# Twenty more score banks on VectorE, early memsets and a new instruction order in a two-layer attention and mixer kernel

## The chip, the cores and the metric

The kernel runs on one core of a Trainium2 chip. The metric is device time in microseconds (us) of one execution; the median of several executions is given. Five engines work side by side, each through its own list of instructions in order, and wait for each other by semaphores: PE (TensorE, matmuls; PEld is its weight load), ACT (ScalarE), DVE (VectorE), POOL (GpSimd) and SP (SyncE, which here only issues DMAs).

## The reference

The same layer is applied twice to a 2048 x 448 matrix: attention with 16 heads of 28 columns, then a mixer of two small feed-forward steps.

```python
def _A_ref(x, wqkv, wo):                 # S = 2048, D = 448, H = 16, Dh = 28
    qkv = (x @ wqkv).reshape(B, S, 3, H, Dh).transpose(2, 0, 3, 1, 4)
    q, k, v = qkv[0], qkv[1], qkv[2]
    p = softmax(einsum("bhqd,bhkd->bhqk", q, k) * Dh ** -0.5)
    return einsum("bhqk,bhkd->bhqd", p, v).transpose(0, 2, 1, 3).reshape(B, S, D) @ wo

def _B_ref(x, w1, w2, w3, w4):
    h = gelu(layernorm(x) @ w1)
    # four column groups of h, shifted by -1, +1, -2, +2 rows, side by side: hs
    x1 = x + hs @ w2
    return x1 + gelu(layernorm(x1) @ w3) @ w4     # w3: 448 x 1792

for _ in range(2):
    x = x + _A_ref(layernorm(x), wqkv, wo)
    x = x + _B_ref(layernorm(x), w1, w2, w3, w4)
```

## The kernel before

**Tiling.** The 2048 rows are 16 tiles of 128. The attention goes by *units* of 512 query columns: four in the first layer, three of 512 and two of 256 in the second. A unit is worked off in *segments*, one for each of four groups of four heads (the first unit of layer 0 and the first two of layer 1 also go by three parts of the keys). The work of a segment is cut into *score banks*: a PSUM bank with 128 keys by 512 scores of one head. PE fills a bank with scores (`L1441`, K=32 rows, one matmul, or two of 256 columns in the halved units), the exponential of the bank is taken, and PE multiplies it with V (`L1511`) into one accumulating bank. There are 2048 banks in the two layers.

**Two ways for the exponential.** Most banks go to ACT, three and two banks in turn to one ACTIVATE (a *granule*, `L1484`, 128x1536 and 128x1024). Five of the eight PSUM banks hold scores for ACT, so PE can be at most one granule ahead of it. The table `SHARE` says how many banks of each segment go to DVE instead: `t_ditem` computes their exponential with five instructions (`L1396`, `L1402`, `L1407`, `L1409`, `L1412`), from a score bank made by `L1392` to a bf16 tile `dT`. `SHARE` has 116 of the 2048 banks.

**Everything else lies between.** LayerNorm (statistics on DVE, `rstd` on POOL), K, Q and V projections (`wk_pad`, `wq_pad`, `wv`), the norms of q and k (`sq` with `astat`; the squares mostly on POOL, `L1105`), the output projection (`wo_pad`), and the mixer (`w` with `xT` is w1 or w3, `w` with `hT` is w2, `w` with `h2T` is w4) are split into strips of 32 output rows on PE (`Columns.matmul`, `L174`), so that four of them run side by side in the array. Gelu (`L1674`, `L1817`) is on ACT and needs another function table than the exponential, so a table load stands before and after each block of gelus. Filler matmuls (`wk_pad` with `zero` or `ident`) keep PE's clock up.

**What sets the order.** The program is written as some hundred Python generators that yield operations. A list scheduler (`Sched`) lays each engine's instructions in one fixed order, from its own table of durations: a first pass gives each operation a latest start, which is its rank; `reorder` shifts ranks at random by the entries of `SEEDS`, a list of numbers and tuples (about 1050 entries), and a second pass picks by these ranks. On the chip each engine then runs its list in order; only semaphores make it wait. A change in `SEEDS` therefore moves instructions everywhere, and none of its entries can be read by itself.

**The start.** The input is loaded twice: a bf16 copy in a weight buffer (`w`), for the first four tiles, and `x_res` (`L866`, four DMAs from POOL's queue: POOL itself issues them). For the first four tiles DVE computes statistics (`L984`, `L986`, `L990`), POOL `rstd` (`L992`), DVE the normalized rows `xn` (`L1075`), PE transposes them. `t_setup2` (`L957` to `L969`) clears buffers on POOL: `xn` pads, `vaug` (the padded V with its column of ones), `wo_pad`, and the last rows of `w1` and `w3`. The maximum of the norms (`L930` to `L939`, `sc`) is needed before the scaled q (`L1134`). The first ACT exponential follows.

## Time and profile before

| what | us |
|---|---|
| median of 3 runs | 1063.17 (1063.0 to 1063.62) |
| profiled execution | 1062.37 |
| its span on the core | 1060.3 |
| first exponential on ACT starts | 33.48 |
| last exponential on ACT ends | 1014.14 |
| ACT busy | 1003.3 |
| PE busy | 986.8 |
| DVE busy | 840.9 |
| POOL busy | 161.2 |

The span is what lies between the first and the last instruction of the profiled execution; its own time is 2.07 us more, and the median of the runs is 0.8 us above that execution. "Busy" counts the time in which an engine executes something other than waits and issues; matmuls are pipelined, so PE's figure is an upper bound of what it needs. In the rows below, the number in front of a timeline row is its start, the next its length; the bracket at its end tells how long the engine had idled and who released it; a row with "x5" is a group of neighbours on one line. A row with "busy, mean ns" is a group over the whole span. Rows of a table by windows have for each engine the busy time in that stretch and, in brackets, the instructions.

### The profile page before, as it was taken

What the parts mean: (1) busy time and instruction counts of PE and PEld (TensorE: products, weight loads), DVE (VectorE), ACT (ScalarE), POOL (GpSimd) and SP (SyncE); (2) the same over time, 40 slices, a digit from 0 to 9 for tenths busy, and PEclk for the clock granted to TensorE, in tenths of its full rate; (3) what the DMA queues carried; (4) which work ended last, traced back from release to release, by engine and by line L of the source; (5) the groups of instructions that cost most, each with busy time, mean ns of one, the idle gap of its engine ahead of it and who ended that gap; (6) DMA issues with size and microseconds to landing.
All of it is one profiled execution on the core that took longest, in us unless ns stands there. A gap on an engine that the chain in (4) does not pass through costs nothing.

```text
span 1060.3 us, 31768 instructions
## 1 busy us (share of the span) xinstructions
PE 986.8 (93%) x14218; PEld 390.6 (37%) x14219; DVE 840.9 (79%) x1854; ACT 1003.3 (95%) x908; POOL 161.2 (15%) x177
## 2 busy tenths in 40 slices
PE   7999999999999998999998999999999999999898
PEld 5333333333333333333334333333333333443355
DVE  8999999999968775754996689999988788545463
ACT  5899999999999999999699999999999999999954
POOL 5220101210202002100332012001112020120111
PEclk9999999999999999999999999999999999999999
DMA  7222060100000000101112222010011010010000
GB/s 203 61 74 74 25 179 22 22 16 2 22 21 22 2 21 23 21 2 42 32 51 67 75 67 72 22 42 21 11 32 37 2 34 12 22 27 25 12 19 23
DMA packets 77103, 41.26 MB, mean 39 GB/s; under 512 B 61288, under 2 KB 70376, under 8 KB 76968
## 3 DMA queue, kind: packets, MB, share of 16 engines
q1 hardware_dynamic: 74856, 35.58, 12.9%
q0 software_dynamic: 2112, 3.67, 1.4%
q8 instruction: 111, 1.82, 0.7%
q14 instruction: 24, 0.20, 0.1%
HBM read 14.20 MB, written 8.13 MB: 21 GB/s over the span
## 4 chain that ended last, share of the span: by engine, by line
ACT 73%; PE 22%; DVE 4%; issue 0%; DMA 0%; POOL 0%; DVEq 0%; ACTq 0%
ACT PT L1484 66%; PE ps L174 11%; PE ps L1441 5%; PE ps L1511 3%; ACT h2T L1817 3%; PE ps L1796 1%; ACT hT L1674 1%; PE ps L1822 1%; ACT L1484 1%; DVE xn L1075 1%; ACT L1674 1%; DVE st L984 0%; DMA w<-in_A_x_dram 0%; DVE qT L1134 0%; DVE sc L935 0%
## 5 line engine op out<-in xcount | busy, mean ns | idle before, releaser
L1484 ACT ACTIVATE PT<-ps 128x1536 bf16<-128x1536 f32 (+1 forms) x775 | 879.5, 1259 | 14.4 <-PE ps L1441 13.0
L1441 PE MATMUL ps<-qT,kT 32*128 32x512 bf16 (+1 forms) x2184 | 303.0, 359 | 30.8 <-ACT PT L1484 24.9
L1511 PE MATMUL ps<-PT,vaug 128*32 128x512 bf16 (+1 forms) x2184 | 233.0, 360 | 5.1 <-ACT PT L1484 3.5
L1441 PEld LDWEIGHTS ps<-qT,kT 32*128 32x128 bf16 x2184 | 76.0, 91 | 253.9 <-ACT PT L1484 147.0
L174 PE MATMUL ps<-xT,w 128*32 128x512 bf16 (+5 forms) x2324 | 150.6, 345 | 1.0 <-DVE h2T L1805 0.4
L1805 DVE CAST h2T<-ps 128x512 bf16<-128x512 f32 (+2 forms) x126 | 73.7, 585 | 40.5 <-PE ps L174 38.2
L1511 PEld LDWEIGHTS ps<-PT,vaug 128*32 128x32 bf16 x2184 | 61.9, 94 | 108.9 <-issue 53.8
L174 PE MATMUL ps<-w,h2T 128*32 128x448 bf16 x1524 | 94.3, 354 | 6.6 <-ACT h2T L1817 3.0
L1396 DVE TENSOR_SCALAR dT<-ps 128x512 f32<-128x512 f32 x116 | 79.1, 684 | 14.8 <-PE ps L1392 11.3
L174 PE MATMUL ps<-wk_pad,zero 128*32 128x256 bf16 x1644 | 81.0, 275 | 0.0
L1407 DVE SCALAR_TENSOR_TENSOR dU<-dF 128x512 f32<-128x512 uint16 x116 | 79.3, 684 | 0.9
L1412 DVE SCALAR_TENSOR_TENSOR dT<-dU,dT 128x512 int32<-128x512 f32 x116 | 79.4, 685 | 0.8
L1409 DVE SCALAR_TENSOR_TENSOR dU<-dF,dU 128x512 f32<-128x512 uint16 x116 | 79.1, 682 | 0.7
L174 PEld LDWEIGHTS ps<-xT,w 128*32 128x32 bf16 (+1 forms) x2324 | 53.0, 95 | 53.2 <-issue 24.6
L1825 DVE SCALAR_TENSOR_TENSOR x_res<-x_res,mst,ps 128x448 f32<-128x448 f32 x32 | 21.6, 678 | 61.2 <-PE ps L174 48.2
L1105 POOL TENSOR_TENSOR sq<-qT 128x512 bf16<-128x512 bf16 (+1 forms) x32 | 31.9, 999 | 248.9 <-DVE qT L1091 191.7
L1764 POOL TENSOR_TENSOR x_res<-x_res,x1b 128x448 f32<-128x448 f32 x31 | 37.2, 1204 | 184.7 <-DVE x1b L1745 183.2
L174 PEld LDWEIGHTS ps<-w,h2T 128*32 128x32 bf16 x1524 | 38.1, 96 | 43.4 <-issue 15.3
L1105 POOL TENSOR_TENSOR sq<-kT 128x512 bf16<-128x512 bf16 (+1 forms) x32 | 31.7, 991 | 137.3 <-DVE kT L1091 90.9
L1402 DVE TENSOR_SCALAR dF<-dT 128x512 uint16<-128x512 uint16 x116 | 48.5, 418 | 0.6
L174 PEld LDWEIGHTS ps<-wk_pad,zero 128*32 128x32 bf16 x1644 | 40.0, 95 | 23.8 <-issue 19.1
L1817 ACT ACTIVATE h2T<-h2T 128x3584 bf16<-128x3584 bf16 (+2 forms) x18 | 46.9, 2605 | 0.3
(172 smaller groups left out, 1189.3 us busy)
## 6 DMA issues: line engine op xcount, KB each, us to landing
uscr<-u_sb SPq DMA_DIRECT2D x24, 256.0 KB, 2.1
uin<-uscr SPq DMA_DIRECT2D x24, 256.0 KB, 2.8
x_res<-in_A_x_dram POOLq DMA_DIRECT2D x4, 896.0 KB, 5.3
out_dram<-uin SPq DMA_DIRECT2D x16, 112.0 KB, 1.7
w<-in_B_w_dram SPq DMA_DIRECT2D x1, 1568.0 KB, 13.4
w<-in_B_w_dram SPq DMA_DIRECT2D x1, 1344.0 KB, 8.6
h2T<-in_A_wqkv_dram SPq DMA_DIRECT2D x2, 336.0 KB, 4.5
xT<-xn SPq DMA_TRANSPOSE x33, 3.7
```

What stands on the lines that cost most here:

```text
L174: return [self.e.matmul(out=out[c:min(c + 32, self.m)], lhsT=lhsT[:, c:min(c + 32, self.m)], rhs=rhs, start=start, stop=stop, tile_positio ...
L1105: yield op("pool", 0.1 + 0.002 * nw, lambda e, si=si: e.tensor_tensor(out=sq[:, si, 0:nw], in0=dst, in1=dst, op=ALU.mult), reads=dkeys, wr ...
L1396: yield op("dve", c_ps(cw), lambda e, b=b: e.tensor_scalar(out=dT[:, s, 0:cw], in0=ps[:, bi(b), 0:cw], scalar1=65536.0 + 127 * 128.0, scal ...
L1402: yield op("dve", c_f2b(cw), lambda e: e.tensor_scalar(out=dF[:, f, 0:cw], in0=dT[:, s, 0:cw].bitcast(U16).rearrange("p (q two) -> p q two ...
L1407: yield op("dve", c_ps(cw), lambda e: e.scalar_tensor_tensor(out=dU[:, v, 0:cw], in0=dF[:, f, 0:cw], scalar=-16384.0, in1=dF[:, f, 0:cw], ...
L1409: yield op("dve", c_ps(cw), lambda e: e.scalar_tensor_tensor(out=dU[:, v, 0:cw], in0=dF[:, f, 0:cw], scalar=EXPD * 16384.0, in1=dU[:, v, 0 ...
L1412: yield op("dve", c_ps(cw), lambda e: e.scalar_tensor_tensor(out=dT[:, s, 0:cw].bitcast(I32), in0=dU[:, v, 0:cw], scalar=EXPC * 2.0 ** -35 ...
L1441: yield op("pe", 0.012 + W / 2400.0, lambda e, bk=bk, r0=32 * j, g=g, kc=kc, q0=q0, W=W, c0=W * h: e.matmul(out=ps[:, bk, c0:c0 + W], lhsT ...
L1484: yield op("act", e_dur(n), lambda e, b0=b0, p0=p0, cnt=cnt, cw=cw: e.activation(out=PT[:, p0:p0 + cnt, 0:cw], in_=ps[:, b0:b0 + cnt, 0:cw ...
L1511: yield op("pe", 0.004 + nt * 0.0133, lambda e, j=j, rhs=rhs, vs=vs, i=i: e.matmul(out=ps[32 * j:32 * j + 32, bi(SUM), 0:128 * nt], lhsT=v ...
L1805: yield op("dve", c_ps(NW), lambda e, fch=fch, b=b: e.tensor_copy(out=h2T[:, fch, hoff:hoff + NW], in_=ps[:, bi(b), 0:NW]), reads=[("ps", ...
L1817: yield op("act", c_act(7 * NW), lambda e, f0=f0: e.activation(out=h2T[:, f0:f0 + 7, hoff:hoff + NW], in_=h2T[:, f0:f0 + 7, hoff:hoff + NW ...
```

## The change

There are four parts. `SHARE` gives one more bank of each segment to DVE in the third unit of both layers, two more in the fourth unit of layer 0 and one more in the fourth (a halved one) of layer 1: 4 + 8 + 4 + 4 = 20 banks, 136 for 116. Three POOL memsets (`vaug` twice, `wo_pad`) move from `t_setup2` into a task of their own, `t_pads`, that is started with the first operations. The tasks that load `x_res` start after the first `xn` rows in the scheduler's order instead of after `rstd`, the clearing of the `xn` pads too, and that of `w1` and `w3` after `RTN` (`L871` of the changed kernel, a step of the maximum of norms); three memsets lose the mark `nolk`, which only the scheduler's model reads. `SEEDS` is replaced by another list, of about 330 entries. The signals are of the scheduler only; on the chip no semaphore is added by them.

```diff
     SEEDS = [
-        (3033793134, 1, 35, -35.9), 510908, 684737, (3033793134, 1, 0, -0.4), (3017015515, 1, 0, -39.1), 562618, 531615, 486769, 672476,
...
+        229462, 345458, 889503, (3033793134, 1, 0, -1.6), 467902, 545934, 474656, (3000237896, 1, 0, 32.7), 711263, 951096, 905249, 9256,
...
-    SHARE = {0: {(0, 0): 0, (0, 1): 1, (0, 2): 3, 1: 6, 2: 4, 3: 2}, 1: {(0, 0): 0, (0, 1): 1, (0, 2): 3, (1, 0): 0, (1, 1): 1, (1, 2): 3, 2: 4, 3: 1, 4: 0}}
+    SHARE = {0: {(0, 0): 0, (0, 1): 1, (0, 2): 3, 1: 6, 2: 5, 3: 4}, 1: {(0, 0): 0, (0, 1): 1, (0, 2): 3, (1, 0): 0, (1, 1): 1, (1, 2): 3, 2: 5, 3: 2, 4: 0}}
...
             yield ("spawn", t_warm(), 2)
+            yield ("spawn", t_pads(), 2)
             yield ("spawn", t_load(ld_x, last), 2)
...
+        def t_pads():
+            yield op("pool", 1.2, lambda e: e.memset(vaug[:, :, :].rearrange("p t (h r) -> p t h r", r=32)[:, :, :, 28:32], 0.0), writes=[("vaug_all",)], nolk=1)
+            yield op("pool", 1.5, lambda e: e.memset(vaug[:, :, :].rearrange("p t (h r) -> p t h r", r=32)[:, :, :, 28:29], 1.0), writes=[("vaug_all",)], nolk=1)
+            yield ("sig", ("vinit",))
+            yield op("pool", 1.9, lambda e: e.memset(wo_pad[:, :, :], 0.0), writes=[("wo_pad",)], nolk=1)
...
         def t_load(ld_x, after):
-            yield ("wait", ("rstd0",))
+            yield ("wait", ("xn0",))
...
         def t_setup2():
             yield op("dve", 0.3, lambda e: e.memset(wv[64:128, 3, :], 0.0), writes=[("wvz",)])
-            yield op("pool", 0.55, lambda e: e.memset(xn[:, :, D:512], 0.0), writes=[("xnpad",)], nolk=1)
-            yield op("pool", 1.2, lambda e: e.memset(vaug[:, :, :]...[:, :, :, 28:32], 0.0), writes=[("vaug_all",)], nolk=1)
-            yield op("pool", 1.5, lambda e: e.memset(vaug[:, :, :]...[:, :, :, 28:29], 1.0), writes=[("vaug_all",)], nolk=1)
-            yield ("sig", ("vinit",))
-            yield op("pool", 1.9, lambda e: e.memset(wo_pad[:, :, :], 0.0), writes=[("wo_pad",)], nolk=1)
+            yield ("wait", ("xn0",))
+            yield op("pool", 0.55, lambda e: e.memset(xn[:, :, D:512], 0.0), writes=[("xnpad",)])
...
-            yield op("pool", 0.5, lambda e: e.memset(w1[:, 3, :], 0.0), writes=[("w1z",), ("w1",)], nolk=1)
-            yield ("wait", ("acol",))
-            yield op("pool", 1.9, lambda e: e.memset(w3[:, 3, :], 0.0), writes=[("w3z",), ("w3",)], nolk=1)
+            yield ("wait", ("rtn",))
+            yield op("pool", 0.5, lambda e: e.memset(w1[:, 3, :], 0.0), writes=[("w1z",), ("w1",)])
+            yield op("pool", 1.9, lambda e: e.memset(w3[:, 3, :], 0.0), writes=[("w3z",), ("w3",)])
...
-            if L == 0 and c == 0:
-                yield ("sig", ("rstd0",))
-            yield from norm_x(tiles, xs, L == 0 and c == 0)
+            yield from norm_x(tiles, xs, L == 0 and c == 0)
+            if L == 0 and c == 0:
+                yield ("sig", ("xn0",))
```

Lines behind the list of `SEEDS` stand 65 to 69 lower in the changed kernel: `L1441` is `L1376` there, `L1484` is `L1419`, `L1511` is `L1446`, `L1817` is `L1752`, `L1075` is `L1010`, `L992` is `L927`, `L866` is `L797`.

What the new order moves is shown at three places. In these rows a bracket names the semaphores that the instruction waits for, and "x12" is a run of like rows.

First POOL's list at the start, before, from the affine selects that make the identity:

```order
L886 AFFINE_SELECT e<-ones_f 128x4 x2
L992 TENSOR_TENSOR rstd<-vpe,neghalf 128x2 [waits sem_dve]
L957 MEMSET xn 128x8x64
L958 MEMSET vaug 128x320x4
L992 TENSOR_TENSOR rstd<-vpe,neghalf 128x2 [waits sem_dve]
L866 DMA x_res<-in_A_x_dram 128x4x448 [waits dma10]
L959 MEMSET vaug 128x320 [waits sem_pool]
L866 DMA x_res<-in_A_x_dram 128x4x448 x2
L961 MEMSET wo_pad 128x1792
```

and the same place of the changed kernel, up to the memsets of `w1` and `w3` (both named `w` here):

```order
L817 AFFINE_SELECT e<-ones_f 128x4 x2
L875 MEMSET vaug 128x320x4
L876 MEMSET vaug 128x320 [waits sem_pool]
L878 MEMSET wo_pad 128x1792
L927 TENSOR_TENSOR rstd<-vpe,neghalf 128x2 [waits sem_dve] x2
L797 DMA x_res<-in_A_x_dram 128x4x448 [waits dma10]
L797 DMA x_res<-in_A_x_dram 128x4x448 x2
L896 MEMSET xn 128x8x64
L797 DMA x_res<-in_A_x_dram 128x4x448
...
L927 TENSOR_TENSOR rstd<-vpe,neghalf 128x4 [waits sem_dve]
L903 MEMSET w 128x448
L904 MEMSET w 128x1792
```

Three memsets have gone ahead of both `rstd`; the DMA issues stand together right behind the second one, and the memsets of `w` behind the third.

Second PE's list at the end of layer 0. Before, the w4 matmuls of the third unit's mixer (`w,h2T`) lie in runs of 4 to 16 between the last scores of the layer; the last score of layer 0 is the last `L1441` row:

```order
L1511 MATMUL ps<-PT,vaug 32x512 x5
L174 MATMUL ps<-w,h2T 32x448 x4
L1511 MATMUL ps<-PT,vaug 32x512 [waits sem_act]
L1511 MATMUL ps<-PT,vaug 32x512 x2
L1441 MATMUL ps<-qT,kT 128x512 x3
L174 MATMUL ps<-w,h2T 32x448 x16
L1441 MATMUL ps<-qT,kT 128x512 [waits sem_act]
L1441 MATMUL ps<-qT,kT 128x512
L174 MATMUL ps<-w,h2T 32x448 x4
L174 MATMUL ps<-xT,wq_pad 32x512 [waits sem_dve]
L174 MATMUL ps<-xT,wq_pad 32x512 x3
L1441 MATMUL ps<-qT,kT 128x512 [waits sem_act]
```

In the changed kernel the last score of layer 0 (the first `L1376` row) comes first, and all of that w4 work behind it, ahead of the first score of layer 1 (which is the last row):

```order
L174 MATMUL ps<-xT,wk_pad 32x512 x12
L174 MATMUL ps<-wv,xT 32x448 x12
L1376 MATMUL ps<-qT,kT 128x512 [waits sem_act]
...
L174 MATMUL ps<-xT,wq_pad 32x512 x15
L174 MATMUL ps<-w,h2T 32x448 [waits sem_dve,sem_act]
L174 MATMUL ps<-w,h2T 32x448 x27
...
L174 MATMUL ps<-w,h2T 32x448 x67
...
L174 MATMUL ps<-sq,astat 32x512 [waits sem_dve,sem_pool]
L174 MATMUL ps<-sq,astat 32x512 x3
L1376 MATMUL ps<-qT,kT 128x512 [waits sem_dve,sem_act]
```

Between these two scores lie 224 w4 matmuls, 64 of `wq_pad`, 32 of `sq` and 16 of `wv`; before, 60 of `wq_pad`, 32 of `wk_pad`, 12 of `sq` and 16 of `wv`. ACT's gelus that make this `h2T` stand four banks ahead of the layer's last exponential now, and 36 banks ahead of it before.

Third PE's list in the fourth unit of layer 1. Before, the w3 matmuls (`xT,w`, 32x512) are spread in runs of 4 to 12 between the scores:

```order
L1441 MATMUL ps<-qT,kT 128x256 x5
L174 MATMUL ps<-xT,w 32x512 x4
L1563 MATMUL ps<-rT,selq 128x128 [waits sem_dve]
L1563 MATMUL ps<-rT,selq 128x128
L1441 MATMUL ps<-qT,kT 128x256 [waits sem_act]
L1441 MATMUL ps<-qT,kT 128x256 x3
L1511 MATMUL ps<-PT,vaug 32x256 x9
L174 MATMUL ps<-xT,w 32x512 [waits sem_dve]
L174 MATMUL ps<-xT,w 32x512 x7
```

Now they come in two runs of 64 between granules five banks apart, of which this is the first:

```order
L1376 MATMUL ps<-qT,kT 128x256 x5
L1446 MATMUL ps<-PT,vaug 32x256 x4
L174 MATMUL ps<-xT,w 32x512 [waits sem_dve]
L174 MATMUL ps<-xT,w 32x512 x11
L174 MATMUL ps<-xT,w 32x512 [waits sem_dve]
L174 MATMUL ps<-xT,w 32x512 x19
L1446 MATMUL ps<-PT,vaug 32x256 x12
L174 MATMUL ps<-xT,w 32x512 [waits sem_dve]
L174 MATMUL ps<-xT,w 32x512 x11
L174 MATMUL ps<-xT,w 32x512 [waits sem_dve]
L174 MATMUL ps<-xT,w 32x512 x19
L1376 MATMUL ps<-qT,kT 128x256 [waits sem_act]
```

Two other runs of this kind are new: ahead of the 1012th score matmul (the 64th of layer 1), 28 of `wq_pad`, 16 of `sq` and 64 of w1 without a score between; and some 40 to 100 scores later three runs of 48, 64 and 80 w3 matmuls of 256 columns (before: runs of 32 to 48 at that place).

More of the change, by code (lines that the diff above doesn't have):

```diff
@@ L956, in t_setup2 @@
             yield op("dve", 0.3, lambda e: e.memset(wv[64:128, 3, :], 0.0), writes=[("wvz",)])
-            yield op("pool", 0.55, lambda e: e.memset(xn[:, :, D:512], 0.0), writes=[("xnpad",)], nolk=1)
-            yield op("pool", 1.2, lambda e: e.memset(vaug[:, :, :].rearrange("p t (h r) -> p t h r", r=32)[:, :, :, 28:32], 0.0), writes=[("vaug_all",)], nolk=1)
-            yield op("pool", 1.5, lambda e: e.memset(vaug[:, :, :].rearrange("p t (h r) -> p t h r", r=32)[:, :, :, 28:29], 1.0), writes=[("vaug_all",)], nolk=1)
-            yield ("sig", ("vinit",))
-            yield op("pool", 1.9, lambda e: e.memset(wo_pad[:, :, :], 0.0), writes=[("wo_pad",)], nolk=1)
+            yield ("wait", ("xn0",))
+            yield op("pool", 0.55, lambda e: e.memset(xn[:, :, D:512], 0.0), writes=[("xnpad",)])
             yield op("dve", 0.1, lambda e: e.memset(zero[:, :], 0.0), writes=[("zero",)])
```

117 rows, old and new, of the table SEEDS are left out of this document.

## The prediction

> **What bounds the kernel now.** I read the page's busy times and its chain of waits first, then the windows, then ACT's timeline for its gaps, and PE's timeline beside them.
>
> ```profile
> PE 986.8 (93%) x14218; PEld 390.6 (37%) x14219; DVE 840.9 (79%) x1854; ACT 1003.3 (95%) x908; POOL 161.2 (15%) x177
> ACT 73%; PE 22%; DVE 4%; issue 0%; DMA 0%; POOL 0%; DVEq 0%; ACTq 0%
> L1484 ACT ACTIVATE PT<-ps 128x1536 bf16<-128x1536 f32 (+1 forms) x775 | 879.5, 1259 | 14.4 <-PE ps L1441 13.0
> ```
>
> ACT carries the chain. Its exponentials are 879.5 us for 2048 - 116 = 1932 banks, 0.455 us a bank. Where it idles before one, PE's scores are late: 13.0 of 14.4 us. So ACT sets the end, and PE, 93% busy, is the next limit: whatever is put between two scores on PE shows as an ACT gap once the granule that PE is ahead is used up. The whole is start (33.48 us to the first exponential) + ACT's work and gaps (to 1014.14) + a tail.
>
> ```profile
> 200.00:300.00 100.00, 93.73 (x1231) 32.81 (x1219) 94.79 (x192) 99.99 (x90) 16.19 (x16) 1.00 0.07 16
> 255.00:380.00 125.00, 117.45 (x1570) 40.80 (x1568) 101.55 (x204) 124.91 (x108) 13.88 (x14) 1.00 0.06 14
> 380.00:512.00 132.00, 125.06 (x1795) 44.49 (x1794) 82.79 (x183) 123.98 (x102) 19.27 (x21) 1.00 0.13 26
> 755.00:880.00 125.00, 117.66 (x1619) 43.23 (x1615) 106.33 (x224) 124.65 (x106) 20.41 (x22) 1.00 0.10 22
> 880.00:945.00 65.00, 59.91 (x1114) 26.75 (x1114) 40.13 (x102) 64.66 (x53) 11.18 (x14) 1.00 0.10 22
> 1014.14:1060.30 46.16, 40.60 (x590) 27.93 (x586) 24.18 (x64) 20.78 (x58) 7.46 (x10) 1.00 0.07 21
> ```
>
> Columns: window and length, then busy time of PE, PEld, DVE, ACT, POOL. The second to fifth rows are about the third and fourth unit of each layer, where the change adds banks; the last is the tail.
>
> **Term 1, the exponentials.** Twenty banks leave ACT: 20 x 0.455 = -9.1 us. On DVE one bank costs
>
> ```profile
> L1396 DVE TENSOR_SCALAR dT<-ps 128x512 f32<-128x512 f32 x116 | 79.1, 684 | 14.8 <-PE ps L1392 11.3
> L1407 DVE SCALAR_TENSOR_TENSOR dU<-dF 128x512 f32<-128x512 uint16 x116 | 79.3, 684 | 0.9
> L1412 DVE SCALAR_TENSOR_TENSOR dT<-dU,dT 128x512 int32<-128x512 f32 x116 | 79.4, 685 | 0.8
> L1409 DVE SCALAR_TENSOR_TENSOR dU<-dF,dU 128x512 f32<-128x512 uint16 x116 | 79.1, 682 | 0.7
> L1402 DVE TENSOR_SCALAR dF<-dT 128x512 uint16<-128x512 uint16 x116 | 48.5, 418 | 0.6
> ```
>
> (79.1 + 79.3 + 79.4 + 79.1 + 48.5) / 116 = 3.15 us; 20 banks are +63 us. By unit that is 12.6, 25.2, 12.6 and 12.6 us, against free DVE time of 125 - 101.55 = 23.5, 49.2, 18.7 and 24.9 us in the windows above. The tightest comes to 119 of about 123 us, the others to 93% and less; at 94.8% (200 to 300 us) ACT was still busy for 99.99 of 100. So I cost it at nothing; with the cover gone, the third unit of layer 1 alone would give back some 4 us. PE's work for a bank is the same either way.
>
> **Term 2, the start.** DVE's `xn` rows and a step of the norms are held up while POOL works:
>
> ```profile
> 9.61 5.27 DVE L1075 TENSOR_SCALAR xn<-w,mv,rstd 128x448 bf16<-128x448 bf16 x2 [0.41 <-POOL rstd L992]
> 8.31 0.89 DVE L1075 TENSOR_SCALAR xn<-w,mv,rstd 128x448 bf16<-128x448 bf16 x2
> 7.13 0.53 POOL L957 MEMSET xn<- 128x512 bf16 x1
> 7.59 1.17 POOL L958 MEMSET vaug<- 128x1280 bf16 x1
> 9.53 0.97 POOL L866 DMA_DIRECT2D x_res<-in_A_x_dram  x1
> 10.49 1.54 POOL L959 MEMSET vaug<- 128x320 bf16 x1
> 11.61 1.51 POOL L866 DMA_DIRECT2D x_res<-in_A_x_dram  x2
> 13.08 1.66 POOL L961 MEMSET wo_pad<- 128x1792 bf16 x1
> 19.06 2.69 DVE L935 TENSOR_SCALAR sc<-sc,cols 128x4 f32<-128x4 f32 x1
> 20.11 1.61 POOL L969 MEMSET w<- 128x1792 bf16 x1
> 33.48 2.36 ACT L1484 ACTIVATE PT<-ps 128x1536 bf16<-128x1536 f32 x2 [0.64 <-PE ps L1441]
> ```
>
> Two rows cost 0.89 us undisturbed and 5.27 us here: 4.4 us lost, the third until the DMA issues end (13.12), the fourth until the `wo_pad` memset does (14.74). The changed order takes the memsets away from there, but not the DMA issues: 0.97 + 0.75 x 3 and the 0.53 us memset of `xn`, from about 9.1, end at 12.9; the two rows then end at about 13.3 to 13.5 instead of 14.88, 1.4 us earlier; if the issues hold up nothing, 4.4. The 2.5 us of `L935` end with POOL's memset of `w`; that memset now follows the third `rstd`, and another such step (`L871`) stands beside it on DVE, so I count no gain, with 2.5 as the bound. The early memsets take 1.17 + 1.54 + 1.66 = 4.4 us from 1.8 and so end at 6.2, just ahead of the first `rstd`, which ran ahead of the 7.13 row; a loss bound of 1.5 if they run longer. With the earlier third DMA I take -2.0 (bounds -6.9 and +1.5).
>
> The Trainium skill, page "SBUF — State Buffer", section "Who interferes with whom", says that VectorE and GpSimd share one port pair, which the instruction that starts first holds to its end while the other blocks wholly. The trace agrees where two rows of 0.89 us together last 5.27, and by that rule the start would gain only as far as the DMA issues let go, the -1.4 above.
>
> Behind the 15th score the new order puts 12 `wk`, 12 `sq` and 28 `wv` matmuls in one run; by the rule of the next part 52 x 0.06 - 1.25 = 1.9 us of ACT gap if nothing else is waited for there, none if ACT waits for its q anyway: +1.2.
>
> **Term 3, runs on PE between scores.** The trace prices such a run. ACT's gaps around the change of layers:
>
> ```profile
> 512.41 12.60 ACT L1484 ACTIVATE PT<-ps 128x1024 bf16<-128x1024 f32 x11 [8.10 <-PE ps L1441]
> 526.48 5.97 ACT L1484 ACTIVATE PT<-ps 128x1536 bf16<-128x1536 f32 x5 [1.46 <-PE ps L1441]
> 545.61 1.02 ACT L1484 ACTIVATE PT<-ps 128x1024 bf16<-128x1024 f32 x1 [0.79 <-PE ps L1441]
> 566.41 3.28 ACT L1484 ACTIVATE PT<-ps 128x1024 bf16<-128x1024 f32 x3 [0.23 <-PE ps L1441]
> 570.07 4.70 ACT L1484 ACTIVATE PT<-ps 128x1536 bf16<-128x1536 f32 x4 [0.37 <-PE ps L1441]
> 480.16 6.41 ACT L1817 ACTIVATE h2T<-h2T 128x3584 bf16<-128x3584 bf16 x2
> 478.87 1.28 ACT L1817 ACT_TABLE_LOAD   x1
> ```
>
> and what PE did ahead of them:
>
> ```profile
> 484.18 5.12 PE L174 MATMUL ps<-w,h2T 128*32 128x448 bf16 x100 [0.20 <-DVE kmaxc L1118]
> 503.38 1.69 PE L174 MATMUL ps<-xT,wq_pad 128*32 128x512 bf16 x28
> 543.34 1.91 PE L174 MATMUL ps<-xT,w 128*32 128x512 bf16 x32
> 564.54 1.08 PE L174 MATMUL ps<-xT,w 128*32 128x256 bf16 x32
> 936.91 1.51 PE L174 MATMUL ps<-w,h2T 128*32 128x448 bf16 x28
> 940.41 21.99 ACT L1484 ACTIVATE PT<-ps 128x1024 bf16<-128x1024 f32 x19 [0.17 <-PE ps L1441]
> ```
>
> The run of 32 matmuls at 543.34 (1.91 us, 0.060 each) gives the gap of 0.79 at 545.61; runs of 1.1 to 1.5 us cost 0.2 (564.54 the gap at 566.41, the last two rows 0.17). I take a run to cost its length less 1.25. A 256-column matmul takes 1.08 / 32 = 0.034, a w4 matmul 5.12 / 100 = 0.051. With these prices, for the changed order:
>
> - Change of layers. Between the last score of layer 0 and the first of layer 1: 224 x 0.051 + 64 x 0.06 + 32 x 0.06 + 16 x 0.06 = 18.1 us, plus up to 2 for squares from POOL. It runs beside ACT's gelus (6.41 + 2 x 1.28 = 8.97). Gap 18.1 + 1.9 - 9.0 - 1.5 = 9.5 (7.9 to 12), for 8.10 before: +1.4. Moving the w4 work behind the scores costs little, because the gelus cover half of it.
> - Layer 1's onset. 28 `wq`, 16 `sq`, 64 w1 in one run: 6.5 us, gap 5.2 (the gelu behind it waits for this w1 and covers nothing). Runs of 48, 64, 80 w3 of 256 columns: 1.6, 2.2, 2.7 us with PV matmuls beside the first and third, gaps 0.4 + 1.0 + 1.6. Three of 20 to 28 with 384 columns: together 1.0. Sum 9.2, for 1.46 + 0.79 + 0.23 + 0.37 = 2.9 before: +6.3.
> - Fourth unit of layer 1. Two runs of 64 w3 with 16 PV matmuls (4.4 us), five banks apart, so that nothing is caught up between them: 2 x 3.15. Four runs of 1.8 to 2.4 behind: 0.7 + 0.4 + 0.7. That is 8.1, for 0.17 before (the last row above). I take +6.5, since ACT may still have granules to work off when the first begins.
>
> Below, a run costs nothing that starts while ACT is behind PE anyway: I bound the 15.4 us of new gaps (1.2 + 1.4 + 6.3 + 6.5) from below by a third of it, 5, and from above by 22, where DVE casts and POOL squares, for which these runs wait, are late as well.
>
> **Term 4, the tail.** Behind the last score the new order has 87 w4 matmuls of 128 columns and 32 of a quarter, where before it was 55 and 104; 32 quarters weigh 8 full ones, so 95 against 81. A full one takes four times 0.051: 14 x 0.2 = 2.8 us more, against a little less of other work. +1.0 (-1 to +4).
>
> **The sum.** -9.1 - 2.0 + 1.2 + 1.4 + 6.3 + 6.5 + 1.0 = +5.3 us on the profiled execution of 1062.37: 1067.7, and the median of the runs stood 0.8 above that execution: 1068, rounded down. So I forecast **slower**: the time taken from ACT comes back as waits for PE.
>
> **The rivals.**
>
> *The runs are absorbed (faster).* The price per run is from gaps where PE was one granule ahead. If PE's runs fall where ACT is behind, because its exponential waits for a `PT` buffer that a PV matmul has to release, they cost nothing. For it: 2.1 us of PE work for five banks at 936 to 946 cost 0.17. Against it: at 543 a run of 1.9 us cost 0.79, with the buffers as they are now. It decides when the new gaps stay under 10 us. With 5 us, no tail term and -3 at the start: 1062.4 - 9.1 - 3 + 5 + 0.8 = 1056. The Trainium skill, page "Perfetto Trace Analysis", section "Optimization Strategy" with the one before it, says to work on the engine with the highest occupancy first; by that rule alone, taking work from ACT (95%) would give 1063.2 - 9.1 = 1054, and this rival is that reading.
>
> *DVE becomes the bound (slower).* Three `dT` buffers feed PE's PV matmuls; if a DVE bank is late, PV waits, `PT` is not freed and ACT stands still. For: 119 of 123 us in the third unit of layer 1. Against: 94.8% in 200 to 300 us cost nothing. Some 2 us in each of the four units: 1068 + 8 = 1076.
>
> *The early memsets do nothing at the start (slower).* The stall moves on to `L871` and the first `rstd` is late by 1.5: 1068 + 2 + 1.5, about 1072.
>
> *It cancels.* New gaps of about 10 and nothing in the tail: 1062.4 - 9.1 - 2 + 10 + 0.8 = 1062.
>
> **How the numbers follow.** Forecast 0.42 (own range 1063.5 to 1074), absorbed 0.27, cancels 0.12, DVE 0.10, memsets 0.09. A measurement of this kernel tells from no change what is over about 0.2%, 2.1 us. Faster: absorbed and a little of cancels, 0.29; within: most of cancels and the forecast's low end, 0.14; slower 0.57. The range is 1055 to 1077: down to the absorbed case with a point of its spread, up to the DVE case.
>
> **What would show it.** ACT's exponential group at 870 us for 1912 banks; DVE busy at 904; the first exponential at 30 to 32 us, with `xn` rows still stretched beside the DMA issues; a gap of 8 to 12 us at the change of layers, one of about 5 some 25 us behind it, and two of about 3 in the fourth unit of layer 1, all released by PE's score line. Gaps before exponentials that sum to 25 us or more mean that I am right; under 20, the first rival. Gaps of PE released by `dT` would mean the second. A first exponential after 33 would mean the third. I am wrong as a whole if ACT has no longer gaps than now.

## The result, and the profile after

The changed kernel took 1073.72 us (median of 4 runs, 1073.28 to 1074.85) beside 1063.09 for the kernel before: a ratio of 1.0102, with a 95% interval of 1.009 to 1.0114. It is slower, by about 10.6 us where 5 were forecast. The profiled execution took 1073.28, its span 1071.4: 11.1 us more than before.

The page of the changed kernel: busy times, the chain of waits by engine, and the group of ScalarE's (ACT's) exponentials.

```profile
PE 996.3 (93%) x14366; PEld 397.6 (37%) x14366; DVE 889.1 (83%) x1958; ACT 991.7 (93%) x895; POOL 164.1 (15%) x177
ACT 74%; PE 21%; DVE 4%; DMA 1%; issue 1%; POOL 0%; DVEq 0%; ACTq 0%
L1419 ACT ACTIVATE PT<-ps 128x1536 bf16<-128x1536 f32 x766 | 870.1, 1268 | 39.1 <-PE ps L1376 38.2 <-PE ps L1446 0.4
```

The exponentials fell by 9.4 us, as they should, and ACT's wait for scores rose from 13.0 to 38.2 (0.6 and 2.0 of these are ahead of the first exponential). Where the long ones are, from ACT's timeline, with the first exponential in the first row and the last in the last:

```profile
29.74 1.45 ACT L1419 ACTIVATE PT<-ps 128x1536 bf16<-128x1536 f32 x1 [2.00 <-PE ps L1376]
41.66 22.30 ACT L1419 ACTIVATE PT<-ps 128x1536 bf16<-128x1536 f32 x20 [4.38 <-PE ps L1376]
511.39 9.14 ACT L1419 ACTIVATE PT<-ps 128x1536 bf16<-128x1536 f32 x8 [11.77 <-PE ps L1376]
548.56 1.02 ACT L1419 ACTIVATE PT<-ps 128x1024 bf16<-128x1024 f32 x1 [7.45 <-PE ps L1376]
915.55 2.37 ACT L1419 ACTIVATE PT<-ps 128x1024 bf16<-128x1024 f32 x2 [2.66 <-PE ps L1376]
920.40 2.37 ACT L1419 ACTIVATE PT<-ps 128x1024 bf16<-128x1024 f32 x2 [2.48 <-PE ps L1376]
1015.94 7.38 ACT L1419 ACTIVATE PT<-ps 128x1024 bf16<-128x1024 f32 x7
```

The span can be added up from this without a rest. "Gaps" are here and below ACT's idle times of 0.15 us or more between the first and the last exponential. They went from 13.0 to 36.7, +23.6. ACT's time between these two exponentials less the gaps fell by 10.7 (9.4 of it the exponentials). The first exponential came 3.7 earlier (33.48 to 29.74). The tail went from 46.16 to 48.08, +1.9. Together +11.1. The gaps by place:

| place | before | after | more | forecast |
|---|---|---|---|---|
| first units (to 80 us) | 0.5 | 5.3 | +4.8 | +1.2 |
| change of layers | 8.1 | 11.8 | +3.7 | +1.4 |
| onset of layer 1 (to 645 us) | 4.2 | 11.9 | +7.7 | +6.3 |
| fourth unit of layer 1 | 0.2 | 7.5 | +7.3 | +6.5 |

In the third units, where VectorE (DVE) got some of its extra banks, next to nothing waits for it (windows; columns as in the prediction's table by windows):

```profile
255.00:380.00 125.00, 116.26 (x1542) 40.42 (x1543) 111.70 (x227) 124.75 (x108) 14.55 (x14) 1.00 0.09 14
755.00:880.00 125.00, 113.53 (x1646) 43.40 (x1648) 110.08 (x235) 124.82 (x108) 20.37 (x22) 1.00 0.09 18
```

In the first of them DVE is busy for 111.70 of 125 us and ACT for 124.75. The extra banks themselves run for nothing there; they are paid for elsewhere.

What sets the first exponential of layer 1 shows in the chain of waits, taken for the change of layers and for the place 37 us behind it (start, length, what):

```profile
491.89 13.44 PE ps L174 x264
505.35 0.69 DVE x_res L1760
506.07 0.63 DVE st L919
506.69 1.19 DVE qT L1022 x2
507.88 1.35 DVE qT L1069 x2
...
511.02 0.35 PE ps L1376 x3
511.39 6.89 ACT PT L1419 x6
...
540.42 0.69 DVE qT L1022
541.24 0.66 DVE qT L1069
...
543.62 0.64 DVE kmaxc L1053
544.30 3.87 PE ps L174 x47
548.17 0.36 PE ps L1376 x2
548.56 1.02 ACT PT L1419
```

On this chain TensorE's (PE's) work and DVE's lie one behind the other: 13.4 us of matmuls, 5.1 of DVE rows, then the scores; further on 3.8 us of DVE rows (540.42 to 544.26), then 3.9 of matmuls. The prediction added up the matmuls, with 1.9 us for POOL's squares at the change of layers, and counted nothing for DVE's rows.

What ACT still had to do at the change of layers, while PE was in that run, between the last score of layer 0 and the first of layer 1 (first and last row):

```profile
489.76 0.39 PE L1376 MATMUL ps<-qT,kT 32*128 32x512 bf16 x1
489.96 6.41 ACT L1752 ACTIVATE h2T<-h2T 128x3584 bf16<-128x3584 bf16 x2
497.68 1.94 ACT L1419 ACTIVATE PT<-ps 128x1536 bf16<-128x1536 f32 x2
510.95 0.60 PE L1376 MATMUL ps<-qT,kT 32*128 32x512 bf16 x5
```

The one ends at 490.15 and the other starts at 510.95, 20.8 us later. Of these ACT covers 9.5, up to 499.62.

### The profile page after: what moved, and what is told of

It reads as the page before. It is cut to its first block, busy times and chain, and to the rows that moved or that the text cites. A ratio compares the mean times of both kernels' runs of the same rounds, so it can differ in the third digit from the quotient of the medians.

```text
span 1071.4 us, 32153 instructions
## 1 busy us (share of the span) xinstructions
PE 996.3 (93%) x14366; PEld 397.6 (37%) x14366; DVE 889.1 (83%) x1958; ACT 991.7 (93%) x895; POOL 164.1 (15%) x177
## 4 chain that ended last, share of the span: by engine, by line
ACT 74%; PE 21%; DVE 4%; DMA 1%; issue 1%; POOL 0%; DVEq 0%; ACTq 0%
ACT PT L1419 66%; PE ps L174 10%; PE ps L1376 4%; ACT h2T L1752 4%; PE ps L1446 3%; PE ps L1757 2%; PE ps L1731 2%; ACT hT L1609 1%; ACT L1419 1%; ACT L1609 1%; DMA x_res<-in_A_x_dram 0%; DVE st L919 0%; DVE qT L1069 0%; DVE kT L1026 0%; DVE h2T L1740 0%
## 5 line engine op out<-in xcount | busy, mean ns | idle before, releaser
L1419 ACT ACTIVATE PT<-ps 128x1536 bf16<-128x1536 f32 x766 | 870.1, 1268 | 39.1 <-PE ps L1376 38.2
L1376 PE MATMUL ps<-qT,kT 32*128 32x512 bf16 (+1 forms) x2160 | 299.6, 359 | 34.8 <-ACT PT L1419 30.3
L1446 PE MATMUL ps<-PT,vaug 128*32 128x512 bf16 (+1 forms) x2160 | 237.1, 361 | 5.1 <-ACT PT L1419 3.9
L1376 PEld LDWEIGHTS ps<-qT,kT 32*128 32x128 bf16 x2160 | 75.8, 91 | 248.3 <-ACT PT L1419 148.8
L174 PE MATMUL ps<-xT,w 128*32 128x512 bf16 (+3 forms) x2140 | 142.7, 354 | 1.6 <-DVE h2T L1740 1.1
L1331 DVE TENSOR_SCALAR dT<-ps 128x512 f32<-128x512 f32 x136 | 92.5, 685 | 16.5 <-PE ps L1327 14.2
L1446 PEld LDWEIGHTS ps<-PT,vaug 128*32 128x32 bf16 x2160 | 60.6, 94 | 116.8 <-issue 56.2
L1342 DVE SCALAR_TENSOR_TENSOR dU<-dF 128x512 f32<-128x512 uint16 x136 | 93.0, 684 | 1.0
L1344 DVE SCALAR_TENSOR_TENSOR dU<-dF,dU 128x512 f32<-128x512 uint16 x136 | 92.8, 683 | 0.8
L1347 DVE SCALAR_TENSOR_TENSOR dT<-dU,dT 128x512 int32<-128x512 f32 x136 | 92.9, 683 | 0.7
L174 PE MATMUL ps<-wk_pad,zero 128*32 128x256 bf16 x1948 | 91.4, 275 | 0.0
L1337 DVE TENSOR_SCALAR dF<-dT 128x512 uint16<-128x512 uint16 x136 | 57.6, 423 | 0.7
L1446 PE MATMUL ps<-dT,vaug 128*32 128x512 bf16 (+1 forms) x144 | 55.2, 391 | 0.0
L1327 PE MATMUL ps<-qT,kT 32*128 32x512 bf16 (+1 forms) x144 | 51.0, 370 | 1.1 <-DVE x1b L1680 0.3
## 6 DMA issues: line engine op xcount, KB each, us to landing
w<-in_B_w_dram SPq DMA_DIRECT2D x1, 1568.0 KB, 15.6
w<-in_B_w_dram SPq DMA_DIRECT2D x1, 1344.0 KB, 10.5
```

Of the source, the lines that this page charges most:

```text
L174: return [self.e.matmul(out=out[c:min(c + 32, self.m)], lhsT=lhsT[:, c:min(c + 32, self.m)], rhs=rhs, start=start, stop=stop, tile_positio ...
L1327: yield op("pe", 0.012 + W / 2400.0, lambda e, kc=kc, h=h, b=b: e.matmul(out=ps[:, bi(b), W * h:W * h + W], lhsT=kT[r0:r0 + 32, g, kc:kc + ...
L1331: yield op("dve", c_ps(cw), lambda e, b=b: e.tensor_scalar(out=dT[:, s, 0:cw], in0=ps[:, bi(b), 0:cw], scalar1=65536.0 + 127 * 128.0, scal ...
L1337: yield op("dve", c_f2b(cw), lambda e: e.tensor_scalar(out=dF[:, f, 0:cw], in0=dT[:, s, 0:cw].bitcast(U16).rearrange("p (q two) -> p q two ...
L1342: yield op("dve", c_ps(cw), lambda e: e.scalar_tensor_tensor(out=dU[:, v, 0:cw], in0=dF[:, f, 0:cw], scalar=-16384.0, in1=dF[:, f, 0:cw], ...
L1344: yield op("dve", c_ps(cw), lambda e: e.scalar_tensor_tensor(out=dU[:, v, 0:cw], in0=dF[:, f, 0:cw], scalar=EXPD * 16384.0, in1=dU[:, v, 0 ...
```

## The experiments

"Exponential" means ACT's `PT` rows throughout. Where no interval is given, a kernel ran once; the kernel before took 1062.2 to 1064.0 us in all its runs. The changed kernel and those of runs 4 to 10 have the same instructions up to the first exponential, and yet it started anywhere from 29.74 to 31.15 in them; so single runs are compared by their gaps rather than by their times.

**1. The memsets alone**, in the kernel before, on POOL's list only:

```diff
  AFFINE_SELECT e (L886)
+ MEMSET vaug (L958); MEMSET vaug (L959); MEMSET wo_pad (L961)
  TENSOR_TENSOR rstd (L992)
  MEMSET xn (L957)
- MEMSET vaug (L958)
...
```

> The kernel before, with its three memsets of vaug and wo_pad moved ahead of the first rstd in POOL's list; no other engine's list differs. As the prediction had it (the third xn row is held by the DMA issues, the fourth by the wo_pad memset): the xn rows end at about 13.4 us instead of 14.88, the first exponential starts near 32 instead of 33.48, the time falls by 1 to 2 us. Rival (the memsets alone hold the rows, the DMA issues nothing): the rows end at about 10.2, the first exponential starts at 29.5 to 30.5, the time falls by 3 to 4 us, to about 1059.5. If the start has no slack to give at all (another chain is as late): under 0.5 us.

1060.47 us, ratio 0.9978 (0.9969 to 0.9988): the best of all kernels here. The two `xn` rows ran through beside three DMA issues (a row of DVE, a row of POOL):

```profile
9.26 0.97 DVE L1075 TENSOR_SCALAR xn<-w,mv,rstd 128x448 bf16<-128x448 bf16 x2 [0.29 <-POOL rstd L992]
9.18 2.46 POOL L866 DMA_DIRECT2D x_res<-in_A_x_dram  x3
31.51 1.45 ACT L1484 ACTIVATE PT<-ps 128x1536 bf16<-128x1536 f32 x1 [0.64 <-PE ps L1441]
```

They ended at 10.23 instead of 14.88, but of these 4.65 us only 1.97 reached the first exponential. The gaps behind it stayed at 13.0.

**2. The memsets of `w` too.** As 1, with those behind the third `rstd`, so that `L935` should not be held up.

> The kernel before with the three early memsets as in the run that moved them alone, and the two memsets of w1 and w3 put behind the third rstd in POOL's list; nothing else differs. In that run the step of the norms on L935 still took 2.69 us beside POOL's DMA issue and these memsets. If the memsets hold it: L935 takes 0.2, the first exponential starts about 2 us earlier (29 to 30 us) and the time falls to 1057.5 to 1059. If the DMA issue ahead of them holds it, or if the first exponential hangs on something else by then: within 0.5 us of 1060.5.

1060.78, ratio 0.998 (0.9971 to 0.9989). `L935` now took 0.21 us instead of 2.69, and the first exponential came at 31.59: no earlier. The stall was real and on no path that counts; counting nothing for it was right.

**3. Runs of zero matmuls** put between scores of the kernel before, one run at a place, to price a run:

```diff
+    sites = {404: 2, 459: 8, 494: 16, 554: 32, 719: 4, 1230: 8, 1268: 16, 1300: 32, 1440: 64}
```

Behind so many scores stand so many groups of four matmuls: runs of 8 to 256.

> The kernel before, with filler matmuls (256 columns, 0.034 us each) added at nine quiet places between scores: 8, 32, 64, 128 and 16 in layer 0 and 32, 64, 128 and 256 in layer 1, which is 0.3, 1.1, 2.2, 4.4, 0.5 and 1.1, 2.2, 4.4, 8.7 us. Price of the prediction (a run costs ACT its length less 1.25 us): gaps of 0, 0, 1, 3.1, 0 and 0, 1, 3.1, 7.5 us, some 16 us in all, a span near 1076. Price without the discount (the run as a whole): the same gaps each about 1 us longer, 22 us in all, a span near 1082. Rival (runs are absorbed, since ACT is behind PE for other reasons): no gap below 4 us, under 8 us in all.

1078.04 us, span 1076.0. The three in layer 0 that showed, and the longest:

```profile
248.19 15.95 ACT L1484 ACTIVATE PT<-ps 128x1536 bf16<-128x1536 f32 x14 [0.35 <-PE ps L1441]
265.29 15.04 ACT L1484 ACTIVATE PT<-ps 128x1536 bf16<-128x1536 f32 x13 [1.14 <-PE ps L1441]
295.24 22.72 ACT L1484 ACTIVATE PT<-ps 128x1536 bf16<-128x1536 f32 x20 [2.69 <-PE ps L1441]
770.70 29.72 ACT L1484 ACTIVATE PT<-ps 128x1536 bf16<-128x1536 f32 x26 [6.42 <-PE ps L1392]
```

At 0.034 us a matmul these runs are 1.1, 2.2, 4.4 and 8.7 us; the gaps are the length less 0.7, 1.0, 1.7 and 2.3. The runs of 64 and 128 in layer 1 gave 0.85 and 2.92, 1.3 and 1.4 less than their lengths. The 32 of layer 1 and all shorter runs cost nothing. For a run of nothing but matmuls the price of the prediction (length less 1.25) holds to about 1 us, and none of 64 or more was hidden.

**4. The runs of the changed kernel thinned** to one of their four column strips:

> The changed kernel, in which 120 operations of PE inside its long runs compute one strip of 32 output rows instead of four (the rest of their results is left as it stands in PSUM): all w4 of the run at the change of layers (168 matmuls less, 8.5 us), wq and w1 of the run ahead of the 1012th score (60 less, 3.6 us), w3 of three runs in the fourth unit of layer 1 (120 less, 2.9, 2.9 and 1.4 us), wv of the run behind the 15th score (12 less, 0.7 us). Nothing else differs on any engine. If PE's work in the runs makes the gaps: the gap at the change of layers falls from 11.8 to 3 to 5 us, the one of 7.45 to about 4, those of 2.66 and 2.48 to 0 to 0.3, the one of 4.38 only to 3.7 since most of it is waits for DVE and POOL; some 18 us less, a span near 1054. If the chain of q and k norms over DVE and POOL makes the gaps, as a rival has it: the first stays over 8 us, the second over 6, and the span above 1063.

1073.17, and every gap as in the changed kernel (11.72, 7.41, 2.65 and 2.33 at the large ones). The four strips of 32 columns run side by side, so one takes as long as four; the run took no time away and said nothing on its question.

**5. Work left out of the runs:** 48 w4 steps at the change of layers, 8 of w1, 20 of w3.

> The changed kernel with matmuls left out of its long runs: of each accumulation over w4 at the change of layers only the first and the last of 14 steps are done (192 of 224 matmuls of a strip less, 48 x 0.2 = 9.8 us), of each over w1 ahead of the 1012th score and over w3 in the fourth unit of layer 1 two of four (1.9, 1.9, 1.9 and 0.95 us less). Those sums are not the reference's. If the runs make the gaps: at the change of layers 11.8 falls to 2 to 3 us, 7.45 to 5.5, 2.66 to 0.8 and 2.48 to 0.6, some 15 us less, a span near 1056.5. If the chains of norms over DVE and POOL make them: 11.8 stays above 8, 7.45 above 7, a span above 1064.

1073.47: next to nothing gained. The gap at the change of layers was 12.05, though 192 matmuls were gone. Three other places lost 1.9 us of matmuls each, and their gaps went from 7.45 to 6.94, from 2.66 to 2.23 and from 2.48 to 2.02 only. PE now waited inside the runs; the last two rows are from the fourth unit of layer 1:

```profile
497.80 0.37 PE L174 MATMUL ps<-w,h2T 128*32 128x448 bf16 x4 [1.13 <-ACT h2T L1752]
...
500.72 0.62 PE L174 MATMUL ps<-sq,astat 128*32 128x512 bf16 x4 [1.19 <-DVE x_res L1760]
502.13 1.31 PE L174 MATMUL ps<-w,h2T 128*32 128x448 bf16 x12 [0.79 <-DVE kmaxc L1053]
504.97 3.61 PE L174 MATMUL ps<-xT,wq_pad 128*32 128x512 bf16 x32 [1.53 <-DVE x_res L1760]
...
914.35 0.40 PE L174 MATMUL ps<-xT,w 128*32 128x512 bf16 x4 [0.77 <-DVE h2T L1740]
915.08 0.83 PE L174 MATMUL ps<-xT,w 128*32 128x512 bf16 x12 [0.33 <-DVE h2T L1740]
```

The matmuls were not what the score waited for alone: DVE's rows, which read the results of such a run, are nearly as long as the matmuls in these places. The 32 `wq_pad` took 3.61 us here and 2.01 in the changed kernel; the windows say why (the third number from the end is PE's granted clock):

```profile
495.00:500.00 5.00, 2.10 (x32) 0.47 (x23) 3.11 (x11) 4.97 (x3) 1.04 (x1) 1.00 0.01 3
500.00:505.00 5.00, 1.96 (x20) 0.47 (x24) 4.78 (x13) 1.00 (x2) 2.05 (x2) 0.53 0.00 0
505.00:508.60 3.60, 3.60 (x36) 1.25 (x36) 1.83 (x3) 0.00 (x0) 0.00 (x0) 0.50 0.64 146
```

PE was busy for 2.10 of 5 us, and then its clock went to half, from 500.3 to 510.6; in the changed kernel it is 1.00 throughout this place. So some 1.6 of the 12.05 us are the clock's (an estimate, from the two times of the `wq_pad` row).

**6 and 7. VectorE's rows left out there, and both.** The statistics, aggregation and normalization rows between the last score of layer 0 and the first of layer 1 (eleven, some 4 us), first alone, then with the 48 w4 steps of run 5.

> The changed kernel with eleven VectorE rows left out at the change of layers (four statistics rows, three aggregations, four normalization rows, about 4 us of VectorE's work there), so layer 1 normalizes some tokens wrongly. If the matmuls in the run set when layer 1's first score comes, the 11.8 us gap stays within 0.5 us. If VectorE's rows set it alone, it falls by about 4 us to 8, and the time to about 1069. If both are as long, as the run without 48 w4 steps suggests, the gap falls by 1 to 2 us only, by the statistics rows that stood between the last residual row and the query casts.

> The changed kernel with the eleven VectorE rows and the 48 w4 matmul steps both left out at the change of layers; layer 1 then works on other values. If two chains of like length run side by side there, leaving out both shortens the gap by more than the two single runs together: from 11.8 us to 6 to 8, and the time to 1067 to 1070. If the GELU on ScalarE, which ends 13 to 15 us ahead of the first exponential of layer 1, and the projections behind it set the first score by themselves, the gap stays above 10.

The gap at the change of layers in the four kernels:

| | all DVE rows | eleven DVE rows out |
|---|---|---|
| all w4 steps | 11.77 | 11.38 |
| 48 w4 steps out | 12.05 | 9.79 |

Either alone moves it by 0.4 or less, both by 2.0; the times were 1074.09 and 1071.60. This is what two chains of about equal length side by side would give, of which the longer sets the score. The test is not quite clean, since both kernels without the w4 steps also lost the clock: with 1.6 and 1.4 us taken off for that (the estimate above, and the same for the row below), the w4 steps alone would be worth 1.3 us, the rows 0.4 and both 3.4. That is still more together than apart. What is left with both out starts at ACT's gelu (chain of waits of that kernel):

```profile
488.99 1.28 ACT L1752
...
493.51 3.20 ACT h2T L1752
...
502.49 3.40 PE ps L174 x18
505.92 0.69 DVE qT L1022
...
509.74 5.97 ACT PT L1419 x5
```

From the gelu's end (496.71) to the exponential (509.74) are 13.0 us, of which the slowed `wq_pad` matmuls are 1.4 more than at full clock. For run 6 the 11.38 is the expected case in which the matmuls set the score (within 0.5); for run 7 both expected cases missed on size: under 8 if two chains were all, over 10 if the gelu and what follows it were.

**8. The scores put first.** The changed kernel, the same instructions at the change of layers: the query steps ahead of the w4 steps, and layer 1's first sixteen or so banks between these.

> The changed kernel with the same instructions, at the change of layers in another order on TensorE and VectorE: the query steps of layer 1's first head group are ahead of the w4 steps, and its first sixteen or so score banks stand between those steps instead of behind them. If the place of the w4 run ahead of the scores makes the 11.8 us gap, it falls by 3 to 7 us and the time to about 1066 to 1070. If the chain of residual, normalization and casts over VectorE and GpSimd sets when the first score of layer 1 can run, the gap stays within 1 us of 11.8, or moves behind the first scores, and the time stays within 2 us of 1073.

1086.43, 13 us slower, which neither expected case had. The 11.77 became 3.29 + 11.39, and gaps of 1.6, 5.6 and 1.3 stood behind. The early scores took PE from the w4 steps, whose residual and normalization the next projections wait for. From 521.7 to 535.4 PE's granted clock was 0.50 as well, so the gaps of 5.6 and 1.3 are in part the clock's; the 11.39 stands ahead of that. The gap is not the place of the w4 run alone.

**9 and 10. The gap of 4.38 in the first units.** PE's rows ahead of it, in the changed kernel:

```profile
35.87 0.83 PE L174 MATMUL ps<-xT,wk_pad 128*32 128x512 bf16 x12
...
37.70 0.75 PE L174 MATMUL ps<-wv,xT 128*32 128x448 bf16 x12 [0.78 <-DVE kT L1026]
...
39.74 0.40 PE L174 MATMUL ps<-sq,astat 128*32 128x512 bf16 x4 [0.26 <-DVE bcol L1168]
40.37 0.75 PE L174 MATMUL ps<-wv,xT 128*32 128x448 bf16 x12 [0.23 <-DVE vaug L1086]
41.05 0.60 PE L1376 MATMUL ps<-qT,kT 32*128 32x512 bf16 x5
```

From the last score to the next are 5.2 us; the forecast had 3.1, from matmuls alone. Here the bias steps of the second head group were moved ahead on DVE, alone and with five scores moved forward on PE.

> The changed kernel with only the four DVE steps of the second head group's bias moved ahead, PE's order as it was. If the late bias alone makes the gap of 4.38 us: it falls below 2. If the run of wk, sq and wv matmuls ahead of the scores makes it, with its waits for DVE and POOL: it stays at 3.5 to 4.4, since the scores still stand behind the run.

> The changed kernel with ten instructions moved at the start and nothing else: on DVE the four short steps of the second head group's bias (L1164, L1166, L1168, L1279) come ahead of casts and statistics, and on PE the five scores that follow the gap of 4.38 us are put three behind the wk matmuls and two behind the first wv matmuls of the run. If the gap is made by this chain and by the run that stands ahead of the scores: it falls to 0 to 1.5 us and the time by 2.5 to 4 us, to about 1070. If it hangs on something else (the squares on POOL, the wk cast): it stays above 3 us and the time within 1 us of the changed kernel's.

Alone: 1073.8, the gap 4.80. With the scores: 1074.65, ratio 1.0105 (1.0092 to 1.0119), a gap of 0.76 and one of 3.28 one granule later. The gap only moved to the next scores, since the chain of projections behind it was as late as ever.

**11. The new share with the old list of seeds.**

> The kernel before with the new SHARE alone (136 banks on DVE), its own SEEDS and memsets. The list scheduler lays out a new order. If the twenty banks are good for their 9 us and the rest of the loss is the order of the changed kernel: ACT's exponentials at 870 us, gaps of another size than the 36.7 us of the changed kernel, at other places, and a time anywhere between 1055 and 1075, as the gaps are. If the twenty banks themselves make the gaps (DVE late in the units that got them): gaps in those units again, of 5 us or more, released by dT or by scores behind it, and a time of 1070 or more.

1154.99, ratio 1.0866 (1.0845 to 1.0887). The exponentials fell to 873.3, and the gaps came to 104, the longest of 15.6 us at 684.9. In its chain of waits the rows of DVE's banks (`dT`, `dU`) stand among the casts (`kT`, `vaug`) that the next matmuls wait for:

```profile
679.15 0.60 DVE dT L1396
...
681.33 0.39 DVE kT L1091
681.72 0.60 DVE dU L1407
682.32 0.54 DVE vaug L1151
```

The seeds (848 entries before, 253 in the changed kernel) shift the ranks of one given plan's steps; in another plan the same list is noise. So share and order cannot be taken apart with the lists as they are.

**12. The new seeds and share without the early memsets.**

> The kernel before with the new order and the new share of banks, but the three memsets where they were: the change without its early memsets. If the third and fourth normalization row are held by the memsets, they end near 14.9 us again, the first exponential comes at 32 to 34 us instead of 29.7, and the gap of 4.4 us near 41.7, which waits for the following projections, shrinks or stays by whether these were held too. If the early start is given back in that gap, the time is within 1 us of 1073.3; if the early start is worth its 3.7 us, the time is near 1077.

1100.89, for the same reason as 11: another set of steps at the start makes another plan, and gaps of 15.5, 6.0 and 6.7 us stood far from the memsets. It doesn't price them. The first exponential came at 28.08, the earliest of all, though the `xn` rows ended as late as 13.2: the held-up rows aren't what the first exponential waits for in every order. One of these rows took 1.77 us and ended with two DMA issues behind which a memset stood, so that what holds a row in such a mixture is still open.

**13 to 16. Share without seeds.** With the list emptied the planner's own order remains, and the share can be changed alone: old, new, new in layer 0 only, new in layer 1 only.

> The kernel before with its list of seeds emptied: the planner's own order with the old share. It is the twin of the changed kernel without seeds. Its ScalarE exponentials are expected at 879 us as before, and the gaps ahead of them, 13.0 us in the kernel before, at 30 us or more: what the seeds are worth with the old share. If the changed kernel's seeds are worth less than that, the order and not the share made the 23.6 us of new gaps.

> The changed kernel with the list of seeds emptied: the planner's own order, unswapped, with the 20 extra banks on VectorE. Beside its twin with the old share it prices the share without a hand-made order. If the 20 banks are worth what they take off ScalarE whatever the order, it is about 9 us faster than the twin; if the added exponentials push VectorE's casts behind the matmuls that need them, it is as slow or slower than the twin, with gaps released by TensorE matmuls that waited for VectorE. Both are expected well above 1073.

> The changed kernel without seeds, with the extra banks on VectorE in layer 0 only. Without seeds the new share in both layers had 56.1 us of gaps and the old share 35.7. If the banks make gaps behind their own units, about 9 to 11 us of the 20 appear here, between the third unit of layer 0 and the end of layer 1's onset, and none of the 9 us in the fourth unit of layer 1. If it is the order as a whole, the gaps appear anywhere. Exponentials on ScalarE fall by about 5.6 us to 877.

> The changed kernel without seeds, with the extra banks on VectorE in layer 1 only. If the banks make gaps behind their own units, about 9 us of gaps more than with the old share appear in the fourth unit of layer 1 (about 915 to 965 us), and the change of layers has as little as with the old share. If it is the order as a whole, no such split is seen. Exponentials on ScalarE fall by about 3.8 us to 879.

| extra banks in | time | exponentials | first one at | gaps between |
|---|---|---|---|---|
| neither layer | 1102.16 | 883.0 | 45.1 | 35.7 |
| layer 0 | 1102.28 | 876.8 | 42.3 | 45.1 |
| layer 1 | 1101.29 | 879.7 | 42.2 | 42.0 |
| both | 1108.96 | 873.6 | 42.5 | 56.1 |

The lower three have the early memsets, and with them 2.6 to 2.9 us at the first exponential. In the order nobody tuned, 20 banks take 9.4 us from the exponentials and put 20.4 into gaps; in the tuned pair it is 9.4 and 23.6. By this the banks account for most of the new gaps and the new order for some 3 us; that is an estimate, from single runs in another order. With layer 1's banks alone, the fourth unit of layer 1 gets the long gap that it has with both (this row is with layer 1 alone; with both the gap is 6.32), and with layer 0's alone it has none above 1.2:

```profile
941.49 9.27 ACT L1393 ACTIVATE PT<-ps 128x1536 bf16<-128x1536 f32 x8 [6.31 <-PE ps L1350]
```

The change of layers has the gaps of the kernel with both as soon as layer 0 has its banks, and those of the old share without. With layer 0's banks, 5.3 us of the gaps at the onset of layer 1 are ahead of two ACT rows that wait for DVE itself. Each layer's banks make most of the new gaps behind their own units. The parts add up to 16 of the 20 us only. The reading that fits: ACT goes through its exponentials sooner, and the projections, mixers and normalizations of the next unit, which ran beside the exponentials, still need their time.

## Where the prediction was right, and the step that failed

The span grew by 11.1 us where 5.3 were added up. The 5.8 more are +8.2 in the gaps, +0.9 in the tail, -1.7 at the start and -1.6 in ACT's own time; the last two, 3.3 us to the good, are luck: nothing in the working foresaw them. Of the 8.2 the first units have 3.6, the change of layers 2.3, the onset of layer 1 1.4 and its fourth unit 0.8.

- **Direction and mechanism: right.** The forecast was that ACT's time comes back as waits for PE at the change of layers, at layer 1's onset and in its fourth unit. There most of it came back, released by the score line each time.
- **Term 1, exponentials: right.** -9.1 forecast, -9.4 measured, and no gap above 0.16 us in the windows of the third units. DVE was busy for 889 us, not 904: the banks' five rows rose by 63 us as costed, but other rows fell, those held up at the start among them.
- **Term 2, the start: wrong in a step, and lost again.** The step was that the DMA issues by themselves go on holding the rows, to about 13.3. They did not: the rows ended at 10.2 beside 2.46 us of DMA issues (run 1, and the same in the changed kernel). By the Trainium skill, page "SBUF — State Buffer", section "Who interferes with whom", where VectorE works in a 2-port mode, whoever issues first gets the shared port pair for its whole instruction. The `wo_pad` memset of the kernel before behaves so, these DMA issues did not. The larger gain, 3.7 instead of 2.0 at the first exponential (2.3 to 3.7 in the kernels with the same start), came back as 4.8 us of gaps in the first units. Of the early memsets alone 2.0 of 4.65 us came through.
- **Term 3, runs on PE: the price held, the lengths did not.** The step that failed is that a run is as long as the sum of its matmuls, with nothing for the DVE rows between them. It is wrong where a run has projections in it: 5.2 us for 3.1 in the first units and 8.5 (539.6 to 548.1) for 6.5 at layer 1's onset. There PE waits for DVE's casts before it may go on, and the gaps, 4.38 and 7.45, are about these lengths less 1.25. In the fourth unit of layer 1, where two runs of 4.3 us cost 2.66 and 2.48 (forecast 3.15 each), the sum of the matmuls is right; but DVE's casts are nearly as long there, since half the matmuls left out took only 0.4 us from each gap (run 5). The prediction had late DVE casts only as the upper bound of 22 us for the term; measured were 23.6.
- **The change of layers:** +3.7, not +1.4. The stretch between the scores was 20.8 us for 20.0, ACT covered 9.5 of it for 10.5, and the first exponential stands 0.4 behind its scores. So "the gelus cover half of it" was near the truth, but the sum of matmuls is not all that sets the length: a chain over the gelu, DVE and the projections is about as long, so that taking either away alone frees little (runs 5 to 7).
- **Term 4, the tail:** +1.9 for +1.0, within its bounds; not tested by a run.
- **The rivals.** That the runs are absorbed fell with the gaps of 36.7 and with run 3. That DVE becomes the bound did not happen inside the third units; DVE counts where its casts stand in a chain with PE, which is another thing. That the memsets do nothing fell with run 1. The Trainium skill's rule to work on the most contended engine first (page "Perfetto Trace Analysis", section "Identifying the Most-Contended Engine") gave 1054 here; ACT was relieved by 9.4 us, and the kernel became 10.6 slower.

Open: how much of the gap in the first units and at the onset comes from the banks and how much from the order, which no run took apart in the tuned order; what holds an `xn` row beside DMA issues (run 12); why the two halves without seeds add up to 16 and not 20 us; and whether a list of seeds made for the new share could do better than this one. The best kernel shown is the one before with its three memsets ahead of the norms, 1060.47.

## What to carry to other kernels

An engine that is 95% busy also covers other work; before taking 9 us from it, ask at each unit's end which chain of casts, projections and normalizations ran under that time, and whether it gets shorter too. Price a stretch between two scores by the chain through all engines, from its first input to its last, not by the sum of one engine's instructions. A list of shifts tuned for one plan can be worse than none in another: before 1063, with one table changed 1155, with that table and no list (and the early memsets) 1109.

## What was not expected of the hardware

Matmuls on one of the four 32-column strips of the array take as long as on all four (run 4: no gap moved by more than 0.15 us). A PE that loses its matmuls loses its clock too: with 192 left out of a stretch PE was busy for 2.10 of 5 us, in waits of at most 1.2 us each, and the granted clock then fell from 1.00 to 0.50; 32 `wq_pad` matmuls behind it took 3.61 instead of 2.01 us (run 5, and much the same in run 7). So work taken out of a waiting PE can come back as slower work behind it.
